# Accumulator joins as accumulating GpSimd transfers, two more quarters by block products, and two closings in one unit

## The chip, the cores and the metric

The kernel runs on one core of a Trainium2 chip. TensorE (PE in the profile; PEld is its weight load) multiplies matrices into PSUM, VectorE (DVE), ScalarE (ACT) and GpSimd (POOL) work element by element, and SyncE (SP) issues most transfers. Each engine takes its instructions strictly in the order in which they were written, and waits for semaphores where an instruction needs the result of another engine. The metric is the device time of one execution in microseconds (us).

## The reference

All arrays are bfloat16. `x` is 2048 tokens by 512, there are 32 heads of 128, and 2048 cached keys and values per head. The result is `x` plus the attention output times a gate.

```python
def _A_ref(x, k_cache, v_cache, wq, wo):
    B, Sq, D = x.shape
    H, Dh = 32, 128
    q = (x @ wq).reshape(B, Sq, H, Dh).transpose(0, 2, 1, 3)
    scores = jnp.einsum("bhqd,bhkd->bhqk", q, k_cache) * (Dh ** -0.5)
    p = _softmax(scores, axis=-1)
    o = jnp.einsum("bhqk,bhkd->bhqd", p, v_cache)
    return o.transpose(0, 2, 1, 3).reshape(B, Sq, H * Dh) @ wo
...
x = A_x
xn = _layernorm(x, axis=-1)
s = _A_ref(xn, A_k_cache, A_v_cache, A_wq, A_wo)
g = _silu(_B_ref(xn, B_w1, B_w2, B_w3, B_w4))
return x + s * g
```

`_B_ref` is an MLP mixer over the same tokens. The kernel computes its gate first and stores it in DRAM; the change doesn't touch it.

## The kernel before, in words

**Units and slots.** After the mixer the kernel runs 128 units. A unit is one head on one quarter of the queries (512 of 2048). Heads go in eight groups of four; the order is group, quarter, head, so unit number = 16 x group + 4 x quarter + head. A unit has eight slots. In each slot TensorE computes the scores of 256 keys (two matmuls of 512 columns into `ps_s`), ScalarE takes their exponential (`pT`, L447), and TensorE does the PV product of a slot ten slots back (`ps_o`). Every other piece of work is put at a slot by tables (`steps`, `o_steps`, `o_early`, `todo`) and written there by one loop, so an engine's order is fixed by hand. "117.3" below is slot 3 of unit 117.

**Row sums and normalisation.** VectorE adds up the exponentials of a unit (`add_first` L453, `add_half` L458, `add_next` L462, folds L466 and L470). One half of one addition (L458) is done by GpSimd at slot 6. The sums are turned by a DMA (`tT`), reduced, inverted, stored and broadcast by SP (`dr`, `rb`), and at slot 7 two units later VectorE multiplies `ps_o` by `rb` into `oT` (L524).

**Output projection.** When the four heads of a group are normalised for a quarter, `oT` (512 by 512) is multiplied by four heads' rows of `wo`, and added to f32 accumulators that stay in SBUF. This goes in one of two ways.

- *Direct*: `wo_slot` runs `wo_mm`, four matmuls of 512 columns for each tile of 128 tokens, and `wo_post` adds the PSUM bank `ps_wo` to the accumulator (L668). A quarter has four tiles. The bank is a single one, so the next tile waits for L668. `PLAN` names units in which these slots are set by hand: none in its first unit, then four tiles in three units.
- *Block products*: `wo_product` works on pairs of tiles. Operands are cut in halves both ways, and seven products in place of eight give the pair (`tw` and `so` are sums of weight and operand blocks); each product is two matmuls of 256 columns for 128 rows. `wo_take` adds PSUM to the accumulators four times a pair (L598), `o_sum` makes four operand sums a quarter (L573). `BLOCK` lists the quarters that are done so: of groups 0 to 6 all but the first of group 0 and the last two of group 6.

**Joins.** For block products the accumulators of a pair of tiles are one buffer `sa` of five pieces of 256 columns. Piece 3 holds a term that three of the four results share, summed over all groups. Once the last block product of a quarter is taken, `wo_join` adds piece 3 to pieces 2 and 4 in one VectorE operation and to piece 1 in another (L604). That is done for eight pairs.

**Closing tiles.** The last group's products are direct. For quarters 0 and 1 `fin_load` brings a tile's `x` and gate (`xl`, `gl`) through SP, and after the tile's last addition `y_last` multiplies the accumulator by the gate (L676), adds `x` (L678), and SP stores the tile. One tile is closed at slot 3 of each unit in which one is ready. For quarters 2 and 3 the accumulators are scaled by the gate ahead of the last product: `gate_load` brings the gate into a buffer that is free by then, `y_scale` multiplies (L636), and `y_add` adds `x` by an accumulating transfer of GpSimd from DRAM (L640). `LATER` is the unit after the last block quarter: 104 here. The joins, scalings and `PLAN` are placed relative to it.

Of the kernel before, what the change touches and what calls it, by code (L numbers as in the profile page):

```python
# [9 lines left out]
ALU = mybir.AluOpType  # L10
FP32 = mybir.dt.float32
BF16 = mybir.dt.bfloat16
# [5 lines left out]
def kernel(  # L18
# [15 lines left out]
    nc = tc.nc  # L34
    P = nc.NUM_PARTITIONS
# [3 lines left out]
    Sq, D = x2d.shape  # L39
# [5 lines left out]
    QT = Sq // 512  # L45
# [6 lines left out]
    NG = H // HG  # L52

    SPU = KC // 2
# [34 lines left out]
    qtp = ent(pool("qt", 6))  # L89
# [21 lines left out]
    def mm(out, lhsT, rhs, start, stop, **kw):  # L111
# [9 lines left out]
        out=ident[:], in0=diag[:], scalar1=0.0, scalar2=None, op0=ALU.is_equal))  # L121
# [5 lines left out]
    LATE = (QT - 2, QT - 1)  # L127
# [7 lines left out]
    def at(n, fn):  # L135
        todo[n].append(fn)
# [399 lines left out]
    def halves(x):  # L536
        return x.rearrange("p (a c) -> p a c", a=2)

    def sa_pair(qt, i):
        x = sp[qt, i] = pS.tile([P, 5, D // 2], FP32, tag="sacc", bufs=NT // 2, name="sacc")  # L540
        sacc[4 * qt + i], sacc[4 * qt + i + 2] = x[:, 0:3:2, :], x[:, 1:5:3, :]
        return x
# [5 lines left out]
    def sa_clear(qt, i):  # L548
        pin(nc.gpsimd.memset(sa_pair(qt, i)[:], 0.0))
# [49 lines left out]

    def wo_join(qt, i):  # L600
        sa = sp[qt, i]
        for out in (sa[:, 2:5:2, :], sa[:, 1:2, :]):
            n = 2 if out is not None and out.shape[1] == 2 else 1
            pin(nc.vector.tensor_tensor(  # L604
                out=out, in0=out, in1=sa[:, 3:4, :].to_broadcast([P, n, D // 2]), op=ALU.add))

    def gate_load(t, i):
        tag = ("tw0", "so2", "tw3", "so0", "so1", "so3", "tw1", "tw0")[i]
        gin[t] = pS.tile([P, D], BF16, tag=tag, bufs=2 if tag == "tw0" else 1, name="gin")[:]
        pin(nc.sync.dma_start(out=gin[t], in_=gates[t][:]))  # L610

    wog, sp, tw, so, wo_ps, gin = {}, {}, {}, {}, {}, {}
# [22 lines left out]
    def y_scale(t):  # L635
        pin(nc.vector.scalar_tensor_tensor(  # L636
            out=sacc[t], in0=sacc[t], scalar=0.5, in1=halves(gin[t]), op0=ALU.mult, op1=ALU.mult))

    def y_add(t):
        pin(nc.gpsimd.dma_start(out=sacc[t], in_=halves(xsrc[t]), accum_op=ALU.add))  # L640
# [31 lines left out]
    pair, last = {}, deque()  # L672
# [322 lines left out]
    pS = None  # L995
# [52 lines left out]
    def pv_run(n):  # L1048
        while pv_at[0] <= n - LAG:
            pv_slot(*divmod(pv_at[0], SPU))  # L1050
            pv_at[0] += 1

    def norm_queue(u):
        norm(u)
        gg, qq, hh = units[u]
        if hh == HG - 1 and (gg, qq) not in BLOCK:
            wo_todo.extend((gg, 4 * qq + ts) for ts in range(4))
# [5 lines left out]
    def wo_slot(part, n, each=2, **kw):  # L1063
        gg, t = wo_todo[0]
        if part < HG // each:
            wo_mm(gg, t, tuple(range(part * each, (part + 1) * each)), **kw)
            return
        wo_todo.popleft()
        wo_post(gg, t, n)
        if gg == NG - 1 and t % 4 < 3 and t + 1 not in fin and t // 4 not in LATE:  # L1070
            fin_load(t + 1)

    FIRST, LAST = 14, NU - 4
    BLOCK = [(g, qt) for g in range(NG - 1) for qt in range(QT)][1:-2]
    APART = range(2 * HG, NU - 3)
    pairs = range(FIRST, LAST + 1, 2)
    q_plan = defaultdict(list)
# [12 lines left out]
    o_steps, o_early = defaultdict(list), defaultdict(list)  # L1090
    for g, qt in BLOCK:
        u0 = ((g * QT + qt) * HG + 6) * SPU
# [13 lines left out]
            o_early[u0 + n].append((wo_sum, g, i))  # L1106
    for i, (qt, u) in enumerate((qt, qt * HG + 5 + j) for qt in range(1, QT) for j in range(2)):
        at(u * SPU + 6, lambda qt=qt, i=i: sa_clear(qt, i % 2))
    LATER = (BLOCK[-1][0] * QT + BLOCK[-1][1] + 1) * HG
    for u, qt, i in ((-7, 2, 0), (-4, 2, 1), (0, 3, 0), (1, 3, 1), (6, 0, 0), (10, 0, 1), (12, 1, 0), (14, 1, 1)):  # L1110
        o_steps[(LATER + u) * SPU + 3].append((wo_join, qt, i))
    for i, u in enumerate((10, 11, 12, 13, 14, 16, 18, 20)):
        n = (LATER + u) * SPU
        t = 4 * LATE[0] + i
        at(n - 2 * SPU + 4, lambda t=t, i=i: gate_load(t, i))
        at(n + 3, lambda t=t: y_scale(t))
        at(n + 6, lambda t=t: y_add(t))
    CATCH = {2 * HG * SPU + p: x for p, x in {
        0: ((0, "xa"),), 1: ((1, "xa"),), 2: ((2, "xa"),), 3: ((0, "xm"),), 4: ((1, "xm"),),
        5: ((2, "xm"), (0, "xa")), 6: ((1, "xa"),), 7: ((2, "xa"),)}.items()}  # L1120
    PLAN = {2 * HG: (), LATER + 6: (), LATER + 7: ((2, 0), (3, 1), (7, 2)), LATER + 8: ((1, 0), (3, 1), (4, 2), (6, 0), (7, 1)),
            LATER + 9: ((0, 2), (2, 0), (3, 1), (7, 2))}

# [28 lines left out]
    for n in range(UB * SPU):  # L1152
        u, p = divmod(n, SPU)
        if p == 0 and wo_box and u not in PLAN:
            wo_slot(4, n, each=1)
        s_slot(u, p)
        pv_run(n)
        for v, dcs in q_plan.get(n, ()):
            q_mm(v, dcs)
        run_steps(n, product)  # L1160
        run_steps(n, wo_product)
        run_steps(n, q_take)
        if p == 0 and 1 <= u:
            if u - 2 in TURN:
                turned_sums(u - 2)
                turned_recip(u - 2)
            run_all(o_early, n)
            if u not in third:
                add_last(u - 1)
        if p == 1 and u - 2 in TURN:  # L1170
            bcast(u - 2)
        if p == fold_at(u) and 1 <= u:
            for v in third.get(u, ()):
                add_last(u - 1)
                q_part(v, 1)
# [24 lines left out]
        if p == sum_p and 1 <= u and u - 1 not in TURN:  # L1200
            sums(u - 1)
        if p == sum_p + 1 and 1 <= u and u - 1 not in TURN:
            bcast(u - 1)
        if u == UA and p in (1, 2, 3):
            wo_slot(p - 1, n)
            if p == 3:
                fold_last(u - 1)
        for at_p, part in PLAN.get(u, ()):
            if at_p == p:
                wo_slot(part, n, each=2)  # L1210
        if p in at_wo and u not in PLAN and wo_todo and pS is not None and (p == at_wo[0] or wo_box):
            wo_slot(at_wo.index(p), n, each=each)
        if p == norm_p and u - 2 in TURN:
            norm_queue(u - 2)
        run_steps(n, q_part)
        if p == 4:
            run_all(o_early, n)
            add_first(u)
        run_all(o_steps, n)
        if p == 3 and last:  # L1220
            y_last(last.popleft())
        if p == 6:
            add_half(u, nc.gpsimd, LO) if u in APART else add_next(u, 2)
        pay()
        held_mm(n)
        for fn in todo.pop(n, ()):
            fn()
        if pS is None and not held:
            right.close()
            pS = right.enter_context(pool("pS", side="right", reuse_waits="tile"))  # L1230
            for tag, n in [("tw0", 2)] + [(x, 1) for x in ("tw1", "tw3", "so0", "so1", "so2", "so3")]:
                pS.tile([P, 2, D // 2], BF16, tag=tag, bufs=n, name="room")
            pS.tile([P, 2, 256], BF16, tag="xs", bufs=XS, name="room")
            pS.tile([P, 256], FP32, tag="tq", bufs=3, name="room")
# [3 lines left out]
    n = UB * SPU  # L1238
# [27 lines left out]
    def pv_to(k):  # L1266
# [29 lines left out]
        out=diag[:], in0=diag[:], scalar1=0.0, scalar2=None, op0=ALU.is_equal))  # L1296
# [98 lines left out]
```

## Time and profile before

| what | value |
|---|---|
| median of three runs | 1220.2 us (1220.19 to 1220.27) |
| the profiled execution | 1220.16 us |
| its span, from first to last instruction | 1218.4 us |
| busy: PE, DVE, ACT, POOL | 1207.3, 1103.2, 1096.6, 299.1 us |
| granted TensorE clock | 1.000 |

The page gives busy time per engine, the chain of work that ended last, and groups of instructions with their count, mean duration and the idle time before them. A row of the timeline gives a start, the time until the end, engine, line, operation and tiles; x2 or more means that neighbours of one kind are merged, and a bracket gives the engine's idle time ahead of it and what ended that. Operations overlap at their ends, so sums of durations come out some per cent above busy time.

### The profile page before, as it was taken

The page shows a single profiled execution, that of the slowest core. Times are in us where ns is not written, and L with a number is a line of the kernel's source. Part 1 is how long each engine was busy: PE and PEld are TensorE (multiplying, and loading weights), DVE is VectorE, ACT ScalarE, POOL GpSimd, SP SyncE. Part 2 cuts the span into 40 slices and gives each one's busy share as a digit, 9 for nine tenths or more (in the row PEclk, how much of TensorE's full clock was granted, in tenths as well). Part 3 has the DMA queues.
Part 4 walks back from the last instruction along what each step waited for, and adds up shares of the span by engine and source line. Part 5 has one row for each costly group of instructions (what it writes and reads, how often), then busy time and mean ns, then how long its engine had stood idle before and what let it go on. Part 6 is the DMA issues. An engine that isn't in the chain of part 4 may idle for free.

```text
span 1218.4 us, 18896 instructions
## 1 busy us (share of the span) xinstructions
PE 1207.3 (99%) x6556; PEld 676.8 (56%) x6678; DVE 1103.2 (91%) x1945; ACT 1096.6 (90%) x1241; POOL 299.1 (25%) x222
## 2 busy tenths in 40 slices
PE   9999999999999999999999999999999999999998
PEld 7466444555555555555555555555555555555555
DVE  8855789999999999999999999999999999989997
ACT  5444999999999999999999999999999999999996
POOL 5301001323222222222222222222222222233320
PEclk9999999999999999999999999999999999999999
DMA  8771133544334433344343443343344434445542
GB/s 179 176 158 55 40 70 79 96 93 91 82 87 83 104 69 89 83 96 91 75 87 88 99 78 80 87 98 79 85 87 87 105 66 92 84 102 111 122 113 66
DMA packets 248160, 113.08 MB, mean 93 GB/s; under 512 B 195328, under 2 KB 231296, under 8 KB 248064
## 3 DMA queue, kind: packets, MB, share of 16 engines
q1 hardware_dynamic: 244560, 107.21, 40.9%
q0 software_dynamic: 2944, 4.20, 1.5%
q8 instruction: 52, 0.85, 0.3%
q14 instruction: 44, 0.36, 0.2%
q10 hardware_dynamic: 560, 0.46, 0.1%
HBM read 69.60 MB, written 4.45 MB: 61 GB/s over the span
## 4 chain that ended last, share of the span: by engine, by line
PE 98%; issue 1%; ACT 0%; DVE 0%; DVEq 0%; ACTq 0%
PE ps_s L112 41%; PE ps_o L112 38%; PE ps_q L112 8%; PE ps_wo L112 8%; PE ps_m L112 3%; ACT pT L447 0%; PE ps_warm L112 0%; PE ps_oh L112 0%; DVE y L1257 0%; DVE tm L1250 0%; DVE tb L746 0%; PE ps_w L112 0%; DVEq L1390 0%; PE ps_r L112 0%; PE ps_sum L112 0%
## 5 line engine op out<-in xcount | busy, mean ns | idle before, releaser
L447 ACT ACTIVATE pT<-ps_s 128x1024 bf16<-128x1024 f32 x1016 | 1007.6, 1027 | 49.3 <-PE ps_s L112 23.7
L112 PE MATMUL ps_s<-qT,kT 128*128 128x512 bf16 (+1 forms) x2054 | 606.9, 377 | 0.2
L112 PE MATMUL ps_o<-pT,vb 128*128 128x512 bf16 x1885 | 568.7, 379 | 4.7
L458 POOL TENSOR_TENSOR acc<-acc,pT 128x1024 bf16<-128x1024 bf16 x117 | 248.7, 2126 | 728.7 <-ACT pT L447 357.2
L112 PEld LDWEIGHTS <-vb 128*128 128x128 bf16 x1984 | 194.0, 98 | 216.6
L112 PEld LDWEIGHTS <-kT 128*128 128x128 bf16 x2064 | 231.7, 113 | 93.5 <-issue 1.0
L462 DVE TENSOR_TENSOR acc<-acc,pT 128x2048 bf16<-128x2048 bf16 x137 | 167.7, 1224 | 21.1 <-ACT pT L447 5.1
L453 DVE TENSOR_TENSOR acc<-pT 128x2048 bf16<-128x2048 bf16 x127 | 154.8, 1219 | 8.1 <-ACT pT L447 8.0
L598 DVE TENSOR_TENSOR sacc<-ps_wo,sacc 128x512 f32<-128x512 f32 x200 | 123.4, 617 | 14.1 <-PE ps_wo L112 11.2
L466 DVE TENSOR_TENSOR acc<-acc 128x1024 bf16<-128x1024 bf16 x127 | 87.3, 687 | 2.4
L500 DVE TENSOR_REDUCE sm<-tT 128x4 f32<-128x512 bf16 x124 | 84.0, 677 | 5.3 <-DMA tT<-acc 4.9
L524 DVE TENSOR_TENSOR oT<-ps_o,rb 128x512 bf16<-128x512 f32 x127 | 86.5, 681 | 2.2 <-DMA rb<-dr 1.9
L458 DVE TENSOR_TENSOR acc<-acc,pT 128x1024 bf16<-128x1024 bf16 x117 | 79.8, 682 | 0.0
L112 PEld LDWEIGHTS <-wc 128*128 128x128 bf16 x448 | 43.8, 98 | 52.8
L112 PE MATMUL ps_wo<-wo_h,oT 128*128 128x256 bf16 (+1 forms) x295 | 70.7, 307 | 0.2
L112 PEld LDWEIGHTS <-oT 128*128 128x128 bf16 x428 | 41.6, 98 | 45.6
L301 ACT ACTIVATE h2T<-ps_s 128x1024 bf16<-128x1024 f32 x28 | 28.6, 1022 | 35.1 <-PE ps_s L112 35.1
L112 PEld LDWEIGHTS <-so 128*128 128x128 bf16 x400 | 39.1, 98 | 36.5
L470 DVE TENSOR_TENSOR acc<-acc 128x512 bf16<-128x512 bf16 x127 | 54.0, 425 | 4.3
L112 PEld LDWEIGHTS <-wq_h 128*128 128x128 bf16 x396 | 38.7, 98 | 34.3
L112 PE MATMUL ps_q<-xnT,wq_h 128*128 128x256 bf16 (+1 forms) x270 | 55.6, 291 | 0.1
L112 PEld LDWEIGHTS <-w_sb 128*128 128x128 bf16 x368 | 33.6, 98 | 28.9
(136 smaller groups left out, 934.4 us busy)
## 6 DMA issues: line engine op xcount, KB each, us to landing
rb<-dr SPq DMA_DIRECT2D x127, 256.0 KB, 3.8
vb<-in_A_v_cache_dram SPq DMA_DIRECT2D x62, 256.0 KB, 3.0
wq_h<-in_A_wq_dram SPq DMA_DIRECT2D x32, 128.0 KB, 2.5
wo_h<-in_A_wo_dram SPq DMA_DIRECT2D x32, 128.0 KB, 2.3
w_sb<-in_B_w_dram SPq DMA_DIRECT2D x8, 256.0 KB, 4.9
kT<-in_A_k_cache_dram SPq DMA_TRANSPOSE x128, 2.6
gate<-xall POOLq DMA_DIRECT2D x16, 128.0 KB, 2.8
sacc<-in_A_x_dram POOLq DMA_DIRECT2D x8, 256.0 KB, 4.6
```

Of the source, the lines that this page charges most:

```text
L112: pin(nc.tensor.matmul(out=out, lhsT=lhsT, rhs=rhs, start=start, stop=stop, **kw))
L301: pin(nc.scalar.activation(out=h2[c][:, f], in_=ps[:], func=ACT.Gelu_apprx_tanh))
L447: pin(nc.scalar.activation(out=s["pT"][-1][:, jj:jj + 2, :], in_=sps[:], func=ACT.Exp, scale=SCALE))
L453: pin(nc.vector.tensor_tensor(out=s["acc"][:], in0=s["pT"][0][:], in1=s["pT"][1][:], op=ALU.add))
L458: pin(eng.tensor_tensor(out=a[:, part, :], in0=a[:, part, :], in1=e[:, part, :], op=ALU.add))
L462: pin(nc.vector.tensor_tensor(out=a[:], in0=a[:], in1=st[u]["pT"][i][:], op=ALU.add))
L466: pin(nc.vector.tensor_tensor(out=a[:, 0:2, :], in0=a[:, 0:2, :], in1=a[:, 2:4, :], op=ALU.add))
L470: pin(nc.vector.tensor_tensor(out=a[:, 0, :], in0=a[:, 0, :], in1=a[:, 1, :], op=ALU.add))
L500: pin(nc.vector.tensor_reduce(out=sm[:], in_=s["tT"][:], axis=mybir.AxisListType.X, op=ALU.add))
L524: pin(nc.vector.tensor_tensor(out=to, in0=o, in1=rb, op=ALU.mult))
L598: pin(nc.vector.tensor_tensor(out=out, in0=ps, in1=out, op=ALU.add))
```

## The change

Three things change, and with them places in the tables. `wo_join` issues two accumulating transfers on GpSimd's queue, SBUF to SBUF, where VectorE did two additions. `BLOCK` takes in the last two quarters of group 6, so `LATER` becomes 112 and `PLAN` moves to units 118 to 121. And `y_last` also runs at slot 6 of unit 121. The joins are at units 106 to 119 in the order of quarters (before: 97 to 118). The scalings are at 115 to 124 (before: 114 to 124), with the gate loads two units ahead of them into other free buffers.

```diff
     def wo_join(qt, i):
         sa = sp[qt, i]
-        for out in (sa[:, 2:5:2, :], sa[:, 1:2, :]):
-            n = 2 if out is not None and out.shape[1] == 2 else 1
-            pin(nc.vector.tensor_tensor(
-                out=out, in0=out, in1=sa[:, 3:4, :].to_broadcast([P, n, D // 2]), op=ALU.add))
+        for out, n in ((sa[:, 2:5:2, :], 2), (sa[:, 1:2, :], 1)):
+            pin(nc.gpsimd.dma_start(out=out, in_=sa[:, 3:4, :].to_broadcast([P, n, D // 2]), accum_op=ALU.add))
 
     def gate_load(t, i):
-        tag = ("tw0", "so2", "tw3", "so0", "so1", "so3", "tw1", "tw0")[i]
-        gin[t] = pS.tile([P, D], BF16, tag=tag, bufs=2 if tag == "tw0" else 1, name="gin")[:]
+        tag = ("tw1", "tw3", "tw0", "qT", "qT", "so2", "so0", "so1")[i]
+        pl, n = (qtp, 5) if tag == "qT" else (pS, 2 if tag == "tw0" else 1)
+        gin[t] = pl.tile([P, D], BF16, tag=tag, bufs=n, name="gin")[:]
...
-    BLOCK = [(g, qt) for g in range(NG - 1) for qt in range(QT)][1:-2]
+    BLOCK = [(g, qt) for g in range(NG - 1) for qt in range(QT)][1:]
...
+    JOINS = ((-6, 0, 0), (-4, 0, 1), (-2, 1, 0), (0, 1, 1), (2, 2, 0), (4, 2, 1), (5, 3, 0), (7, 3, 1))
+    SCALES = ((8, 3, 3), (10, 4, 4), (9, 5, 5), (11, 6, 6), (12, 7, 7), (14, 7, 8), (13, 10, 10), (15, 12, 12))
...
-    for u, qt, i in ((-7, 2, 0), (-4, 2, 1), (0, 3, 0), (1, 3, 1), (6, 0, 0), (10, 0, 1), (12, 1, 0), (14, 1, 1)):
+    for u, qt, i in JOINS:
         o_steps[(LATER + u) * SPU + 3].append((wo_join, qt, i))
...
-        if p == 3 and last:
+        if (p == 3 or (u, p) == (LATER + 9, 6)) and last:
             y_last(last.popleft())
```

A row of SCALES is the tile, the unit of its scaling and the unit of its residual transfer, both counted from `LATER`. Lines behind the changed place stand one lower in the changed kernel (L676 is L675, L640 is L639).

TensorE at slots 2 and 3 of unit 111, where the direct tiles of group 6 began. Before, `oT` is the stationary operand and the four heads' `wo_h` stream 512 columns each:

```order
L112 LDWEIGHTS oT_12195
L112 MATMUL ps_wo_12639<-wo_h_10276,oT_12195 128x512
L112 LDWEIGHTS oT_12195
L112 MATMUL ps_wo_12639<-wo_h_10276,oT_12195 128x512
L112 LDWEIGHTS kT_11176
```

Now, at the same place, with the next slot's scores behind it:

```order
L112 LDWEIGHTS oT_12189
L112 MATMUL ps_wo_12639<-wo_h_10276,oT_12189 128x256
L112 LDWEIGHTS oT_12189
L112 MATMUL ps_wo_12639<-wo_h_10276,oT_12189 128x256
L112 LDWEIGHTS kT_11176
L112 MATMUL ps_s_12642<-qT_12369,kT_11176 128x512
L112 LDWEIGHTS kT_11176
L112 MATMUL ps_s_12642<-qT_12369,kT_11176 128x512
```

The direct tile with 512 columns a matmul is gone from here; a block product with 256 columns stands in its place, and the direct tiles of the last group come eight units later.

GpSimd in units 114 to 116. Before, only its half of the row sums (L458) and the residual transfers (L640) stand there, in units 114, 115 and 116:

```order
L458 TENSOR_TENSOR acc_12956<-acc_12956,pT_12951 128x1024
L640 DMA sacc_2900<-in_A_x_dram 128x2x256
L458 TENSOR_TENSOR acc_13053<-acc_13053,pT_13049 128x1024
L640 DMA sacc_3005<-in_A_x_dram 128x2x256
L458 TENSOR_TENSOR acc_13152<-acc_13152,pT_13147 128x1024
```

Now two joins (L603) stand among them, those of quarter 2's two pairs, `sacc_2900` and `sacc_3005`:

```order
L603 DMA sacc_2900<-sacc_2900 128x2x256
L603 DMA sacc_2900<-sacc_2900 128x256
L458 TENSOR_TENSOR acc_12969<-acc_12969,pT_12963 128x1024
L458 TENSOR_TENSOR acc_13071<-acc_13071,pT_13064 128x1024
L639 DMA sacc_2900<-in_A_x_dram 128x2x256
L603 DMA sacc_3005<-sacc_3005 128x2x256
L603 DMA sacc_3005<-sacc_3005 128x256
L458 TENSOR_TENSOR acc_13175<-acc_13175,pT_13171 128x1024
```

The second join stands behind a residual transfer and ahead of the row-sum addition of its unit.

VectorE in unit 121, from slot 4 on. Before, the addition of a tile of the last group (L668) follows the first row sums and the last part of a Q projection:

```order
L453 TENSOR_TENSOR acc<-pT 128x2048
L432 TENSOR_TENSOR qT<-ps_q,tq 128x512
L668 TENSOR_TENSOR sacc<-ps_wo,sacc 128x2x256
L524 TENSOR_TENSOR oT<-ps_o,rb 128x512
L500 TENSOR_REDUCE sm<-tT 128x4
```

Now the second closing of the unit, written at slot 6, stands ahead of that addition:

```order
L453 TENSOR_TENSOR acc<-pT 128x2048
L432 TENSOR_TENSOR qT<-ps_q,tq 128x512
L675 SCALAR_TENSOR_TENSOR gl<-sacc,gl 128x512
L677 TENSOR_TENSOR xl<-gl,xl 128x512
L667 TENSOR_TENSOR sacc<-ps_wo,sacc 128x2x256
L524 TENSOR_TENSOR oT<-ps_o,rb 128x512
```

Two operations have moved in ahead of the one that empties `ps_wo`, and of the normalisation behind it.

More of the change, by code (lines that the diff above doesn't have):

```diff
@@ L1108 @@
         at(u * SPU + 6, lambda qt=qt, i=i: sa_clear(qt, i % 2))
+    JOINS = ((-6, 0, 0), (-4, 0, 1), (-2, 1, 0), (0, 1, 1), (2, 2, 0), (4, 2, 1), (5, 3, 0), (7, 3, 1))
+    SCALES = ((8, 3, 3), (10, 4, 4), (9, 5, 5), (11, 6, 6), (12, 7, 7), (14, 7, 8), (13, 10, 10), (15, 12, 12))
     LATER = (BLOCK[-1][0] * QT + BLOCK[-1][1] + 1) * HG
-    for u, qt, i in ((-7, 2, 0), (-4, 2, 1), (0, 3, 0), (1, 3, 1), (6, 0, 0), (10, 0, 1), (12, 1, 0), (14, 1, 1)):
+    for u, qt, i in JOINS:
         o_steps[(LATER + u) * SPU + 3].append((wo_join, qt, i))
[L1112 to L1117, printed above, removed]
+    for i, (t, u, w) in enumerate(SCALES):
+        at((LATER + u - 2) * SPU + 4, lambda t=t, i=i: gate_load(t, i))
+        at((LATER + u) * SPU + 3, lambda t=t: y_scale(t))
+        at((LATER + w) * SPU + 6, lambda t=t: y_add(t))
     CATCH = {2 * HG * SPU + p: x for p, x in {
```

## The prediction

> **What bounds the kernel now.** I read the page's busy times and its chain first, then the stretch that the change touches (units 110 to 122, about 1053 to 1156 us), engine by engine.
>
> ```profile
> span 1218.4 us, 18896 instructions
> ...
> PE 1207.3 (99%) x6556; PEld 676.8 (56%) x6678; DVE 1103.2 (91%) x1945; ACT 1096.6 (90%) x1241; POOL 299.1 (25%) x222
> ...
> PE 98%; issue 1%; ACT 0%; DVE 0%; DVEq 0%; ACTq 0%
> ```
>
> The chain that ended last is 98% TensorE. A busy PE row is not yet a PE at its peak, since ends of matmuls are modelled, so I take the spacing of starts (TensorE in unit 104; a row with x2 is two matmuls one after the other):
>
> ```profile
> 999.66 0.59 PE L112 MATMUL ps_s<-qT,kT 128*128 128x512 bf16 x2
> 1000.09 0.59 PE L112 MATMUL ps_o<-pT,vb 128*128 128x512 bf16 x2
> 1000.52 0.38 PE L112 MATMUL ps_wo<-tw,oT 128*128 128x256 bf16 x2
> 1000.74 0.59 PE L112 MATMUL ps_s<-qT,kT 128*128 128x512 bf16 x2
> ```
>
> Two 512-column matmuls take 0.43 us from start to start, 0.215 us each; two of 256 columns take 0.22, some 0.11 each. Scores, PV and block product follow each other without a hole. So time goes by columns streamed, and what saves columns saves time.
>
> The second clock is the first copy of each pair of Q projections (`tq`, once in two units, at the same place of the even unit):
>
> ```profile
> 1002.34 0.38 ACT L416 ACTIVATE tq<-ps_q 128x256 f32<-128x256 f32 x1
> 1019.21 0.38 ACT L416 ACTIVATE tq<-ps_q 128x256 f32<-128x256 f32 x1
> ...
> 1052.95 0.38 ACT L416 ACTIVATE tq<-ps_q 128x256 f32<-128x256 f32 x1
> 1069.90 0.41 ACT L416 ACTIVATE tq<-ps_q 128x256 f32<-128x256 f32 x1
> 1087.87 0.41 ACT L416 ACTIVATE tq<-ps_q 128x256 f32<-128x256 f32 x1
> 1156.09 0.38 ACT L416 ACTIVATE tq<-ps_q 128x256 f32<-128x256 f32 x1
> ```
>
> These open units 104, 106, 110, 112, 114 and 122. A pair of units with block products takes 16.87 us, and the next two pairs take 33.74, as much each. The planned stretch (units 111 to 113, four direct tiles pressed together) makes its two pairs 16.95 and 17.97. From unit 110 to unit 122 it is 103.14 us.
>
> **The change, part by part.**
>
> *Two quarters by block products.* A direct quarter is 4 tiles by 4 heads: 16 matmuls of 512 columns, two quarters 32 x 0.215 = 6.88 us. By blocks a quarter is 2 pairs by 7 products by 2 matmuls: 28 of 256 columns, two quarters 56 x 0.11 = 6.16 us, or 56 x 0.1075 = 6.02. The saving is 0.72 to 0.86 us, all on the path.
>
> The clock rows give the same by another way. After the change units 110 to 117 are four pairs with block products, 4 x 16.87 = 67.48; the planned stretch stands at 119 to 121, with the same columns in every slot, so its two pairs again cost 16.95 + 17.97 = 34.92. Together 102.40 against 103.14: -0.74 us. From unit 122 on TensorE's rows are the same in both. I take -0.75.
>
> The Trainium skill speaks against this step. "TensorE: Matmul & The Clock Gate", section "Back-to-back issue gap", gives a sustained stream 81 ns at 128 columns and 131 ns at 512, so that half the columns cost far more than half; an estimate between its figures puts 256 columns at 98 ns, and the step would lose 56 x 0.098 - 32 x 0.131 = 1.3 us. The trace disagrees: 0.215 and 0.11 us in the stream of this very kernel, so the rows decide.
>
> *VectorE's share of it.* Rows by form:
>
> ```profile
> L598 DVE TENSOR_TENSOR sacc<-ps_wo,sacc 128x512 f32<-128x512 f32 x150 | 102.8, 685 | 9.4 <-PE ps_wo L112 7.2
> L598 DVE TENSOR_TENSOR sacc<-ps_wo,sacc 128x256 f32<-128x256 f32 x50 | 20.6, 412 | 4.7 <-PE ps_wo L112 4.0
> L573 DVE TENSOR_TENSOR so<-oT 128x512 bf16<-128x512 bf16 x50 | 19.0, 417 | 0.0
> L668 DVE TENSOR_TENSOR sacc<-ps_wo,sacc 128x512 f32<-128x512 f32 x16 | 11.0, 690 | 3.2 <-PE ps_wo L112 2.9
> ```
>
> Two quarters add 12 x 0.685 + 4 x 0.412 additions and 8 x 0.417 operand sums, 13.2 us, and drop 8 x 0.69 = 5.5.
>
> *The joins.* A join is two VectorE additions; the pair stands as one row:
>
> ```profile
> 1005.71 1.02 DVE L604 TENSOR_TENSOR sacc<-sacc 128x512 f32<-128x512 f32 x2
> ...
> 1013.78 1.02 DVE L604 TENSOR_TENSOR sacc<-sacc 128x512 f32<-128x512 f32 x2
> ```
>
> Eight of them are 8.2 us of VectorE gone, which with the step before leaves it 0.5 us lighter. I give that no gain: both rows lie in the pair from 1002.34 to 1019.21, which takes 16.87 us like the two pairs after it. VectorE had room for a join of 1.02 us beside the block products, so it has room for the scaling of 0.68 us that units 115 to 118 now carry each. In unit 119 two scalings stand together (1.36 us), where the last addition of a block product is just done.
>
> On GpSimd a join becomes two accumulating transfers. The nearest rows are the residual transfers, which accumulate the same 128 x 2 x 256 f32 from DRAM, and the gate stores:
>
> ```profile
> L640 POOL DMA_DIRECT2D sacc<-in_A_x_dram x8: 1061/1080/1156, 1095.7 to 1181.1; - x8
> ...
> DMA to landing us min/median/max: 3.5/4.6/4.8
> ```
> ```profile
> 1095.69 1.16 POOL L640 DMA_DIRECT2D sacc<-in_A_x_dram  x1
> ...
> 1118.68 2.12 POOL L458 TENSOR_TENSOR acc<-acc,pT 128x1024 bf16<-128x1024 bf16 x1 [4.56 <-ACT pT L447]
> ```
> ```profile
> L321 POOL DMA_DIRECT2D gate<-xall x16 | 8.9, 559 | 129.5 <-DVE xall L318 129.2
> ```
>
> So the two issues hold GpSimd between 2 x 0.56 = 1.1 and 2 x 1.16 = 2.3 us; I take 2.2, since both accumulate. Queued behind a join is GpSimd's half of the row-sum addition (L458), and VectorE's next addition waits for that. Where a residual transfer stands in the same unit the idle time before that addition is still 4.56 us at least, so 2.2 fits and the price is 0. Landing, 3.5 to 4.8 us a transfer, is needed by the scaling a unit (over 8 us) later at the earliest: 0 too. If the cover went, a join of 2.2 us would delay VectorE by 2.2.
>
> The Trainium skill, "SBUF — State Buffer", section "SBUF: two separate sides", warns that VectorE can lock GpSimd out while it writes descriptors, 3.1 us for a transfer of 0.62. By that figure a join would hold GpSimd 6.2 us, more than the 4.56. The trace does not show it: the eight issues took 1.06 to 1.16 us beside a busy VectorE.
>
> The transfers share the DMA engines with the broadcast of reciprocals (`rb`), which the normalisation waits for:
>
> ```profile
> DVE oT L524 <- DMA rb<-dr: 1.9, 4, 0.6
> ```
>
> That is 1.9 us in four waits of 127. More of these may come; they delay VectorE, not yet TensorE. I price them at 0.
>
> *Two closings in unit 121.* A closing is two VectorE operations (0.682 and 0.426 by their groups). The planned stretch now meets closings, which it did not in units 111 to 113. The rows of VectorE and TensorE at the old end of that stretch:
>
> ```profile
> L676 DVE SCALAR_TENSOR_TENSOR gl<-sacc,gl 128x512 bf16<-128x512 f32 x8 | 5.5, 682 | 0.0
> L678 DVE TENSOR_TENSOR xl<-gl,xl 128x512 bf16<-128x512 bf16 x8 | 3.4, 426 | 0.3
> ```
> ```profile
> 1082.68 1.23 DVE L453 TENSOR_TENSOR acc<-pT 128x2048 bf16<-128x2048 bf16 x1 [0.57 <-ACT pT L447]
> ...
> 1084.65 0.69 DVE L432 TENSOR_TENSOR qT<-ps_q,tq 128x512 bf16<-128x512 f32 x1 [0.74 <-PE ps_q L112]
> 1085.26 0.68 DVE L668 TENSOR_TENSOR sacc<-ps_wo,sacc 128x512 f32<-128x512 f32 x1
> ...
> 1088.16 0.38 PE L112 MATMUL ps_wo<-wo_h,oT 128*128 128x512 bf16 x1
> ...
> 1090.71 1.02 DVE L604 TENSOR_TENSOR sacc<-sacc 128x512 f32<-128x512 f32 x2
> ...
> 1092.26 1.22 DVE L453 TENSOR_TENSOR acc<-pT 128x2048 bf16<-128x2048 bf16 x1
> ...
> 1093.97 0.69 DVE L668 TENSOR_TENSOR sacc<-ps_wo,sacc 128x512 f32<-128x512 f32 x1 [0.50 <-PE ps_wo L112]
> ...
> 1095.72 0.38 PE L112 MATMUL ps_wo<-wo_h,oT 128*128 128x512 bf16 x1
> ```
>
> TensorE's next tile (1088.16, 1095.72) needs the one PSUM bank that L668 empties. Laid over these rows, the closing of 121.3 (1.1 us) falls into the idle 0.57 and 0.74. That of 121.6 stands ahead of the first L668, which then ends at 1087.04 instead of 1085.94, with 1088.16 needed. By the second L668 the closing of 122.3 has come as well (2.2 us) and the old join (1.0) has gone: 1.2 later, of which 0.5 was idle. It ends at about 1095.4 with 1095.72 needed. Price 0, but only 0.3 us of cover; without it the loss is what VectorE is further behind, an estimate of up to 1.2 us, once.
>
> *Gate loads and order of the scalings.* The loads change buffers that lie idle by then (operand sums and weights last read in unit 118 at the latest), with one exception read in the slot just before; their count is unchanged: 0. On SP the loads for tiles 2 to 4 of the last head group now stand behind the stores of closings in units 120 and 121, and the next unit's reciprocals are queued behind them. A load waits only for a store issued more than a slot earlier, so I give this 0 too and leave the doubt to the first rival.
>
> **Sum.** -0.75 against the profiled execution's 1220.16 us (span 1218.4) gives 1219.4; the median of the runs, 1220.2, stands 0.04 above that execution. What a measurement here can tell from no change I set at 0.2%, 2.44 us; so this forecast is "no change".
>
> **Rivals.**
>
> *Gain eaten near unit 121.* For it: 0.3 us of cover, SP's loads for the closings, `rb` landing later beside the joins. Against it: VectorE's idle time in the same rows. It gives back 0.4 to 1.5 us: 1219.8 to 1221. Still within 0.2%.
>
> *GpSimd too late: slower.* A join's issues hold GpSimd so long that its addition, then VectorE, then TensorE wait. The margins:
>
> ```profile
> 956.57 0.68 DVE L598 TENSOR_TENSOR sacc<-ps_wo,sacc 128x512 f32<-128x512 f32 x1
> ...
> 956.78 2.12 POOL L458 TENSOR_TENSOR acc<-acc,pT 128x1024 bf16<-128x1024 bf16 x1 [5.73 <-DVE acc L453]
> ...
> 958.13 0.38 PE L112 MATMUL ps_wo<-wo_h,so 128*128 128x256 bf16 x2
> ...
> 959.70 1.22 DVE L462 TENSOR_TENSOR acc<-acc,pT 128x2048 bf16<-128x2048 bf16 x1
> ```
>
> GpSimd ends at 958.90, VectorE wants it at 959.70 (0.8 us); L598 ends at 957.25, TensorE wants it at 958.13 (0.9). It decides from 4.56 + 0.8 + 0.9 = 6.3 us a join, against 2.2 expected. At 7 us, eight joins cost about 8 x 0.7 = 5.6, less 0.75: 1225. Against it stand the eight rows of about 1.1 us.
>
> *Half-width matmuls cost more than half.* It turns at 6.88 / 56 = 0.123 us; at 0.16 the loss is 2.1 us, 1222.3. The rows of 0.11 speak against it.
>
> *Faster by over 0.2%.* It would need 2.44 us of TensorE's time where the pairs show none: in the direct pair of units 118 and 119 PE is busy 17.02 of 17.07 us.
>
> ```profile
> 1121.04:1138.11 17.07, 17.02 (x87) 8.88 (x87) 16.31 (x28) 16.25 (x20) 5.83 (x4) 1.00 0.59 123
> ```
>
> **How the numbers follow.** Forecast 0.70; gain eaten 0.17; GpSimd too late 0.08; half-width matmuls, at their price of 2.1 us within the bound, 0.02; faster 0.03. Same: 0.70 + 0.17 + 0.02 = 0.89, of which I move 0.02 to slower and 0.01 to faster for what these rows may not show: same 0.86, slower 0.10, faster 0.04. The range goes from 1219.0 (0.86 saved, and 0.3 for what the pairs hide) to 1221.2, the end of the second case, leaving out the slow one.
>
> **What would show it right or wrong.** Right: the period of `tq` is 16.87 in units 110 to 117, PE's idle time before ps_wo stays near 0, GpSimd's transfer rows are 0.5 to 1.2 us. Wrong: transfer rows over 3 us and VectorE's L462 waiting for POOL; periods over 18 us at units 118 to 122; ps_wo of 256 columns spaced more than 0.123 us.

## The result and the profile after

| kernel | median | runs | ratio to before (95% interval) |
|---|---|---|---|
| before | 1220.23 us | 1220.19 to 1220.29 | |
| changed | 1226.66 us | 1224.62 to 1227.22 | 1.0049 (1.0039 to 1.0059) |

The change makes the kernel slower by 0.49%, some 6 us, and its runs spread over 2.6 us where those of before agree within 0.1 (within 1.2 in the later sets). The forecast was 1219.4. The profiled execution took 1225.65 us. The page of the changed kernel, the same parts as were shown of before, with the queue of GpSimd's transfers (packets, MB, share of the 16 DMA engines):

```profile
span 1223.8 us, 18980 instructions
...
PE 1208.3 (99%) x6580; PEld 677.8 (55%) x6702; DVE 1105.2 (90%) x1945; ACT 1096.9 (90%) x1241; POOL 316.3 (26%) x238
...
q0 software_dynamic: 6272, 7.34, 3.2%
...
PE 91%; DVE 5%; DMA 2%; issue 1%; ACT 0%; DVEq 0%; POOL 0%
```

TensorE was 98% of the chain that ended last; now VectorE and DMA carry 7% of it. Busy PE still reads 99%, which tells nothing. The clock of the pairs, `tq` in units 110 to 122, tells where the time is lost:

```profile
1053.04 0.38 ACT L416 ACTIVATE tq<-ps_q 128x256 f32<-128x256 f32 x1
1069.91 0.38 ACT L416 ACTIVATE tq<-ps_q 128x256 f32<-128x256 f32 x1
1086.78 0.38 ACT L416 ACTIVATE tq<-ps_q 128x256 f32<-128x256 f32 x1
1105.16 0.38 ACT L416 ACTIVATE tq<-ps_q 128x256 f32<-128x256 f32 x1
1123.70 0.38 ACT L416 ACTIVATE tq<-ps_q 128x256 f32<-128x256 f32 x1
1140.66 0.41 ACT L416 ACTIVATE tq<-ps_q 128x256 f32<-128x256 f32 x1
1159.04 0.38 ACT L416 ACTIVATE tq<-ps_q 128x256 f32<-128x256 f32 x1
```

The first two pairs take 16.87 us each, as forecast. The pairs of units 114 and 116 take 18.38 and 18.54 in place of 16.87, that of 120 18.38 in place of 17.97: 3.6 us against the forecast. From unit 122 to the end of the span it is 64.8 us where before has 62.3: another 2.5.

The first long pair has its cause in unit 114. SP's queue and GpSimd's, then VectorE and TensorE of the changed kernel:

```profile
1085.49 1.08 SPq L159 DMA_DIRECT2D vb<-in_A_v_cache_dram  x1
1086.67 0.40 SPq L508 DMA_DIRECT2D dr<-rc  x1
1090.71 0.32 SPq L512 DMA_DIRECT2D rb<-dr  x1
```
```profile
1085.35 2.14 POOL L603 DMA_DIRECT2D sacc<-sacc  x2
```
```profile
1091.28 0.69 DVE L598 TENSOR_TENSOR sacc<-ps_wo,sacc 128x512 f32<-128x512 f32 x1
1094.59 0.69 DVE L524 TENSOR_TENSOR oT<-ps_o,rb 128x512 bf16<-128x512 f32 x1 [2.63 <-DMA rb<-dr]
```
```profile
1100.26 0.38 PE L112 MATMUL ps_q<-xnT,wc 128*128 128x256 bf16 x2 [0.50 <-DVE qT L429]
...
1103.53 0.62 PE L112 MATMUL ps_s<-qT,kT 128*128 128x512 bf16 x2 [0.51 <-DVE qT L432]
```

The join's two transfers go out at 1085.35, a value load at 1085.49, and 1.3 us later the tiny store of the reciprocals, `dr` (2 KB). The broadcast `rb` reads what `dr` wrote, so SP can issue it only when `dr` has landed, at 1090.71, 4.0 us after its issue. `dr`'s median over the kernel is 1.5, but at this place it is long without a join too. SP's queue in the kernel with no joins and the closing at slot 7 (see the experiments):

```profile
1085.81 0.40 SPq L508 DMA_DIRECT2D dr<-rc  x1
1088.94 0.32 SPq L512 DMA_DIRECT2D rb<-dr  x1
```

There `rb` follows `dr` after 3.1 us. Counted from `tq` of unit 112, that kernel issues `dr` at 15.67 us and `rb` at 18.80, the changed one at 16.76 and 20.80. Of the 2.0 us by which `rb` goes out later, 0.9 are `dr`'s landing. The other 1.1 are there before: VectorE has waited 0.78 us for `rb` after the join of unit 112, and the value load's issue takes 1.08 us in place of 0.58.

VectorE stands 2.63 us before the normalisation, and TensorE waits for VectorE's Q copies. The groups of the page show the sum of such waits (before: 1.9 for `rb`, longest 0.6, and 4.9 for `tT`; with no joins 4.1 and 6.2, so the joins are only part of the rise):

```profile
L524 DVE TENSOR_TENSOR oT<-ps_o,rb 128x512 bf16<-128x512 f32 x127 | 86.6, 682 | 6.7 <-DMA rb<-dr 6.4
L500 DVE TENSOR_REDUCE sm<-tT 128x4 f32<-128x512 bf16 x124 | 84.0, 677 | 7.3 <-DMA tT<-acc 7.0
```

The loss behind unit 122 looks different. VectorE, GpSimd and TensorE there, where the second closing of unit 121 stands:

```profile
1157.27 2.29 DVE L675 SCALAR_TENSOR_TENSOR gl<-sacc,gl 128x512 bf16<-128x512 f32 x1
1159.60 0.42 DVE L677 TENSOR_TENSOR xl<-gl,xl 128x512 bf16<-128x512 bf16 x1
1159.94 0.68 DVE L667 TENSOR_TENSOR sacc<-ps_wo,sacc 128x512 f32<-128x512 f32 x1
```
```profile
1156.90 2.11 POOL L458 TENSOR_TENSOR acc<-acc,pT 128x1024 bf16<-128x1024 bf16 x1 [5.78 <-issue]
```
```profile
1160.67 0.38 PE L112 MATMUL ps_wo<-wo_h,oT 128*128 128x512 bf16 x1 [1.13 <-DVE sacc L667]
```

L675 takes 2.29 us where its group took 0.68. It started while GpSimd's half addition ran, and ended 0.55 us after that addition did (1159.56 against 1159.01). L667 came late by the 1.6 us that L675 took longer, and the next direct tile waited 1.13 us for the PSUM bank.

### The profile page after: what moved, and what is told of

Same layout as the page of the kernel before. It is cut to its first block, busy times and chain, and to the rows that moved or that the text cites. A ratio compares the mean times of both kernels' runs of the same rounds, so it can differ in the third digit from the quotient of the medians.

```text
span 1223.8 us, 18980 instructions
## 1 busy us (share of the span) xinstructions
PE 1208.3 (99%) x6580; PEld 677.8 (55%) x6702; DVE 1105.2 (90%) x1945; ACT 1096.9 (90%) x1241; POOL 316.3 (26%) x238
## 3 DMA queue, kind: packets, MB, share of 16 engines
q0 software_dynamic: 6272, 7.34, 3.2%
## 4 chain that ended last, share of the span: by engine, by line
PE 91%; DVE 5%; DMA 2%; issue 1%; ACT 0%; DVEq 0%; POOL 0%
PE ps_s L112 38%; PE ps_o L112 35%; PE ps_q L112 8%; PE ps_wo L112 7%; PE ps_m L112 3%; DMA tT<-acc 1%; DVE acc L462 1%; DVE acc L453 0%; DMA rb<-dr 0%; DVE sm L500 0%; DVE acc L466 0%; DVE acc L458 0%; DVE gl L675 0%; DMA dr<-rc 0%; DVE oT L524 0%
## 5 line engine op out<-in xcount | busy, mean ns | idle before, releaser
L458 POOL TENSOR_TENSOR acc<-acc,pT 128x1024 bf16<-128x1024 bf16 x117 | 248.7, 2126 | 716.0 <-DVE acc L453 368.4
L598 DVE TENSOR_TENSOR sacc<-ps_wo,sacc 128x512 f32<-128x512 f32 x216 | 133.5, 618 | 17.1 <-PE ps_wo L112 13.9
L458 DVE TENSOR_TENSOR acc<-acc,pT 128x1024 bf16<-128x1024 bf16 x117 | 80.1, 685 | 0.0
L112 PEld LDWEIGHTS <-so 128*128 128x128 bf16 x432 | 42.3, 98 | 39.5 <-issue 0.2
L112 PE MATMUL ps_wo<-wo_h,oT 128*128 128x256 bf16 (+1 forms) x279 | 61.7, 296 | 1.6 <-DVE sacc L667 1.1
```

The costliest lines, as they stand in the source:

```text
L112: pin(nc.tensor.matmul(out=out, lhsT=lhsT, rhs=rhs, start=start, stop=stop, **kw))
L458: pin(eng.tensor_tensor(out=a[:, part, :], in0=a[:, part, :], in1=e[:, part, :], op=ALU.add))
L598: pin(nc.vector.tensor_tensor(out=out, in0=ps, in1=out, op=ALU.add))
```

## The experiments

My theory (A) was that the joins' transfers delay the chain `dr`, `rb`, `tT`, and so VectorE and TensorE; the first rival (B) that two closings and the planned stretch crowd VectorE and SP in units 119 to 122. The letters that follow stand in the expectations. There are three sets of four kernels, each with runs of the kernel before beside it. In the table, "114 to 121" is the time from `tq` of unit 114 to that of unit 122 in the profiled execution (forecast 2 x 16.87 + 16.95 + 17.97 = 68.66), "rest" from there to the end of the span (before 62.3).

| kernel | median, us | ratio (95% interval) | 114 to 121 | rest |
|---|---|---|---|---|
| changed | 1226.66 | 1.0049 (1.0039 to 1.0059) | 72.3 | 64.8 |
| joins on VectorE | 1224.17 | 1.0029 (1.0018 to 1.0040) | 71.8 | 63.7 |
| early joins transfers, late on VectorE | 1223.74 | 1.0026 (1.0016 to 1.0037) | 71.0 | 64.3 |
| late joins only, as transfers | 1226.14 | 1.0043 (1.0027 to 1.0060) | 72.2 | 64.8 |
| joins as plain copies | 1223.35 | 1.0022 (1.0013 to 1.0032) | 70.0 | 64.6 |
| joins of few bytes | 1222.67 | 1.0017 (1.0008 to 1.0027) | 68.7 | 64.8 |
| no joins | 1221.13 | 1.0004 (0.9995 to 1.0013) | 68.7 | 63.7 |
| no joins, closing at slot 7 | 1220.04 | 0.9996 (0.9987 to 1.0005) | 68.7 | 62.3 |
| one join, closing at slot 7 | 1220.25 | 0.9999 (0.9990 to 1.0008) | 70.1 | 62.5 |
| closing at slot 7 | 1225.70 | 1.0039 (1.0026 to 1.0053) | 74.2 | 63.3 |
| one closing a unit | 1224.83 | 1.0036 (1.0024 to 1.0049) | 73.1 | 62.3 |
| no scalings in 115 to 118 | 1226.24 | 1.0039 (1.0027 to 1.0052) | 71.3 | 64.3 |
| before, joins as transfers | 1221.13 | 1.0006 (0.9997 to 1.0015) | | 62.3 |

**Joins back on VectorE.**

```diff
         for out, n in ((sa[:, 2:5:2, :], 2), (sa[:, 1:2, :], 1)):
-            pin(nc.gpsimd.dma_start(out=out, in_=sa[:, 3:4, :].to_broadcast([P, n, D // 2]), accum_op=ALU.add))
+            pin(nc.vector.tensor_tensor(
+                out=out, in0=out, in1=sa[:, 3:4, :].to_broadcast([P, n, D // 2]), op=ALU.add))
```

> The changed kernel with its eight joins back as VectorE additions, at the changed kernel's places; blocks, planned stretch and closings as changed. Theory A (the accumulating transfers delay the chain of small transfers dr, rb, tT, and with it VectorE and then TensorE): the loss goes, 1219.4 to 1221.0 us, and the longest wait of L524 for rb is back near 0.6 us (2.6 in the changed kernel). Rival B (two closings and the planned stretch crowd VectorE and SP in units 119 to 122, whoever does the joins): 1225 us or more, since VectorE now has 8.2 us more to do; units 120 and 122 stay above 9.4 us.

Measured 1224.17: between both, nearer to B's 1225, and the longest wait for `rb` is 1.2 us, not 0.6. The transfers are worse than the VectorE additions, but VectorE has no room either: the pairs of units 110 and 112 already take 17.14 and 17.13 us in place of 16.87. TensorE of this kernel, in the pair of unit 116 (19.22 us):

```profile
1112.12 0.38 PE L112 MATMUL ps_wo<-wo_h,so 128*128 128x256 bf16 x2 [0.87 <-DVE sacc L598]
...
1120.55 0.38 PE L112 MATMUL ps_wo<-wo_h,oT 128*128 128x256 bf16 x2 [0.68 <-DVE sacc L598]
```

Here a join stands on VectorE beside a scaling and block products in units 116 and 117, and TensorE waits for a block product's addition.

**The kernel before with transfers for joins, at its old places.**

```diff
-            pin(nc.vector.tensor_tensor(
-                out=out, in0=out, in1=sa[:, 3:4, :].to_broadcast([P, n, D // 2]), op=ALU.add))
+            pin(nc.gpsimd.dma_start(out=out, in_=sa[:, 3:4, :].to_broadcast([P, n, D // 2]), accum_op=ALU.add))
```

> The kernel before with nothing changed but the joins, which become accumulating transfers of GpSimd at their old places (units 97, 100, 104, 105, 110, 114, 116, 118). Theory A: slower than before by 2 to 6 us (1222 to 1226), lost in the units after the joins of 114, 116 and 118, where loads or residual transfers stand beside them; the four joins up to 105 cost nothing. Rival B: 1219.5 to 1220.5 us, as before.

Measured 1221.13, 0.7 us above before, with an interval that takes in no difference. So the same transfers cost almost nothing there, and theory A as written is wrong on its own: they cost where they meet something. VectorE of this kernel in unit 114, whose join falls on direct tiles:

```profile
1094.38 0.69 DVE L666 TENSOR_TENSOR sacc<-ps_wo,sacc 128x512 f32<-128x512 f32 x1 [1.43 <-PE ps_wo L112]
1095.85 0.69 DVE L524 TENSOR_TENSOR oT<-ps_o,rb 128x512 bf16<-128x512 f32 x1 [0.79 <-DMA rb<-dr]
```

`rb` is late here too, by 0.79 (`dr` takes 4.7 us, in the kernel before 3.6), but VectorE had just idled 1.43 us for TensorE: it is ahead, and the wait goes no further. The pair of unit 114 takes 17.01 us, as before.

**One closing a unit.** The kernel leaves out one tile's closing altogether, since the row of closings doesn't catch up.

```diff
-        if (p == 3 or (u, p) == (LATER + 9, 6)) and last:
+        if p == 3 and last:
```

> The changed kernel without the second closing of unit 121 (the tile closes one unit later at slot 3). Theory A: 1224.5 to 1227, at most 1.5 us off the changed kernel, and unit 122 alone is shorter. Rival B: most of the loss goes, 1219.5 to 1222.

Measured 1224.83, 1.8 us below the changed kernel. The rest of the span is back at 62.3, and units 114 to 121 stay long: two losses, not one. That is inside A's range, though a little more than the 1.5 us that A allowed. Since one closing is missing, what its place alone costs can't be read from this kernel.

**Early joins as transfers, late ones on VectorE.**

```diff
+            m = sa[:, 3:4, :].to_broadcast([P, n, D // 2])
+            if qt < 2:
+                pin(nc.gpsimd.dma_start(out=out, in_=m, accum_op=ALU.add))
+            else:
+                pin(nc.vector.tensor_tensor(out=out, in0=out, in1=m, op=ALU.add))
```

> The changed kernel with the joins of quarters 0 and 1 (units 106 to 112) left as transfers of GpSimd, those of quarters 2 and 3 (units 114 to 119) back on VectorE. Theory A in its narrow form (a transfer costs something only where loads or residual transfers stand beside it): within 0.5 us of the kernel with all joins on VectorE, 1219.4 to 1221. A in a wide form (every join costs about the same): half of the loss stays, about 1223. Rival B: 1225 or more.

Measured 1223.74, within 0.5 us of all joins on VectorE as the narrow form says, but not at its 1221. Its pairs up to unit 115 take 16.87 us, that of 116 takes 18.59: the late four on VectorE are what costs there, beside the closing.

**The second closing at slot 7**, behind the two operations of that slot which read PSUM.

```diff
-        if (p == 3 or (u, p) == (LATER + 9, 6)) and last:
+        if (p == 3 or (u, p) == (LATER + 9, 7)) and last:
```

> The changed kernel with the second closing of unit 121 at slot 7 in place of slot 6, behind the addition and the normalisation of that slot, which read PSUM. Theory C (L675 of that closing took 2.29 us in place of 0.68 because it reads two operands of SBUF while GpSimd's half addition L458 runs; it ended 0.55 us after L458 in each kernel so far): it takes 0.7 us again, or little more, and the 1.13 us that TensorE waits for L667 go; 1224.5 to 1225.5 us, 1.2 to 2.2 below the changed kernel. Rival D (a second closing costs by its 1.1 us of VectorE work alone, wherever it stands): within 0.5 us of the changed kernel, 1226 to 1227.

Measured 1225.70, 1 us below the changed kernel. The median alone doesn't decide between C and D, since the intervals overlap and units 114 to 121 came out longer in this execution; the rest of the span, 63.3 in place of 64.8, and the rows do. VectorE and GpSimd at the second closing, of this kernel first, then of the one with no joins and the same slot:

```profile
1160.23 1.10 DVE L675 SCALAR_TENSOR_TENSOR gl<-sacc,gl 128x512 bf16<-128x512 f32 x1
```
```profile
1158.66 2.12 POOL L458 TENSOR_TENSOR acc<-acc,pT 128x1024 bf16<-128x1024 bf16 x1 [5.23 <-ACT pT L447]
```
```profile
1153.06 0.68 DVE L667 TENSOR_TENSOR sacc<-ps_wo,sacc 128x512 f32<-128x512 f32 x1
...
1154.25 0.68 DVE L675 SCALAR_TENSOR_TENSOR gl<-sacc,gl 128x512 bf16<-128x512 f32 x1
```
```profile
1152.24 2.11 POOL L458 TENSOR_TENSOR acc<-acc,pT 128x1024 bf16<-128x1024 bf16 x1 [5.54 <-ACT pT L447]
```

In the first L675 still starts 0.55 us before GpSimd is done and ends 0.55 after it (1161.33 against 1160.78). In the second it starts 0.1 us before GpSimd's end (1154.35), at 1154.25, and takes its 0.68. L667, which reads one operand from PSUM, keeps its 0.68 in the middle of GpSimd's addition. So L675 waits for GpSimd and then still needs some half a microsecond.

The Trainium skill has this rule: "SBUF — State Buffer", section "Who interferes with whom", says that a VectorE instruction with two SBUF inputs contends with a GpSimd instruction that reads SBUF, and that the later one blocks until the first is done. The trace agrees: 2.29, 1.10 and 0.68 us for one and the same operation, by where it starts against L458.

**No joins.** The shared term of the block products is left out of the accumulators.

```diff
-    for u, qt, i in JOINS:
-        o_steps[(LATER + u) * SPU + 3].append((wo_join, qt, i))
```

> The changed kernel with no joins at all, neither on GpSimd nor on VectorE (the shared term of the block products is left out of the accumulators). Theory E (of the loss of 7.2 us against the forecast some 4 to 5 belong to the joins' transfers in the DMA queues, the rest to the closing at slot 6 and to scalings beside block products): 1221.5 to 1222.5. Rival A (all of it the transfers): 1219.4 to 1220.3. Rival F (VectorE is overfull in units 115 to 118 whatever the transfers do): above 1223.5.

Measured 1221.13, ratio 1.0004: the joins' transfers are 0.45% (1.0049 less 1.0004) or 5.5 us of the loss, a little more than E said (the time lies just below E's 1221.5, and above A's 1220.3). Units 114 to 121 take 68.7, to the hundredth what the forecast said without any loss. F is out: VectorE is not overfull by the block products and scalings alone.

**No scalings in units 115 to 118.** Tiles 8 to 11 aren't scaled.

```diff
-        at((LATER + u) * SPU + 3, lambda t=t: y_scale(t))
+        if i > 3:
+            at((LATER + u) * SPU + 3, lambda t=t: y_scale(t))
```

> The changed kernel without the four scalings of units 115 to 118 (tiles 8 to 11 aren't multiplied by half their gate); joins stay as transfers, the closing at slot 6. That is 4 x 0.68 = 2.7 us less VectorE work where the block products of group six run. Theory F (VectorE has no room for them beside block products, so that each late rb or tT goes through to TensorE): 2 to 3 us below the changed kernel, 1223.5 to 1224.7. Rival A (the waits for rb and tT alone decide): at most 0.7 us below, 1226 or more.

Measured 1226.24 (1223.65 to 1226.95): 2.7 us less work on VectorE bring 0.4 at the median, which is A's side. But the five runs spread over 3.3 us, and two of them lie in F's range, so this kernel alone decides little; F is out by the kernel with no joins.

**No joins, second closing at slot 7.** Both edits above together.

> The changed kernel with no joins at all and the second closing at slot 7. If the two causes add up, it stands as far below the kernel with no joins as the closing at slot 7 stands below the changed kernel. Theory E with C: 1219.5 to 1221. Rival F: above 1222, with units 115 to 118 still longer than 34.5 us together (33.74 forecast).

Measured 1220.04, some 1.0 us below the kernel with no joins, as the closing at slot 7 stood 1.0 below the changed kernel: at the medians the two causes add up, though each interval reaches about 1 us either way. The clock of the pairs:

```profile
1053.27 0.38 ACT L416 ACTIVATE tq<-ps_q 128x256 f32<-128x256 f32 x1
...
1087.01 0.38 ACT L416 ACTIVATE tq<-ps_q 128x256 f32<-128x256 f32 x1
1103.88 0.38 ACT L416 ACTIVATE tq<-ps_q 128x256 f32<-128x256 f32 x1
1120.75 0.38 ACT L416 ACTIVATE tq<-ps_q 128x256 f32<-128x256 f32 x1
1137.70 0.40 ACT L416 ACTIVATE tq<-ps_q 128x256 f32<-128x256 f32 x1
1155.67 0.40 ACT L416 ACTIVATE tq<-ps_q 128x256 f32<-128x256 f32 x1
```

102.40 us from unit 110 to 122, which is the number of the forecast for that stretch, with the rest as before (62.3). Its ratio, 0.9996, can't be told from 1.

**Plain copies of the same bytes.** The shared term overwrites the accumulators in place of being added.

```diff
-            pin(nc.gpsimd.dma_start(out=out, in_=sa[:, 3:4, :].to_broadcast([P, n, D // 2]), accum_op=ALU.add))
+            pin(nc.gpsimd.dma_start(out=out, in_=sa[:, 3:4, :].to_broadcast([P, n, D // 2])))
```

> The changed kernel with the joins' transfers as plain copies of the same bytes, without accumulating (so the shared term overwrites the three accumulators in place of being added). Theory A (bytes on the 16 DMA engines delay dr, rb and tT): 1225 to 1227, as the changed kernel. Rival G (the accumulation is what makes them slow; a plain copy has shorter packets and lands sooner): 1221 to 1223.

Measured 1223.35, just above G's range and below A's: plain copies cost 0.18% over no joins (2.2 us), accumulating ones 0.45%. At the medians more than half of the price is the accumulation.

**Few bytes.** Sixteen accumulating transfers of as many pieces, with 16 of 256 columns; the others aren't joined.

```diff
-            pin(nc.gpsimd.dma_start(out=out, in_=sa[:, 3:4, :].to_broadcast([P, n, D // 2]), accum_op=ALU.add))
+            pin(nc.gpsimd.dma_start(out=out[:, :, 0:16], in_=sa[:, 3:4, 0:16].to_broadcast([P, n, 16]), accum_op=ALU.add))
```

> The changed kernel with the same sixteen accumulating transfers, but of 16 columns in place of 256 for each piece (the other 240 columns aren't joined). GpSimd issues as many transfers with as many pieces; the bytes are a sixteenth. Theory A: 1221 to 1222.5, as with no joins. Rival H (what GpSimd does for the issue is the cost, by its own time or by keeping VectorE from SBUF): 1225 to 1227.

Measured 1222.67, just above A's end and far from H's. Units 114 to 121 are back at 68.7 with GpSimd's issues as long as ever. So most of it isn't the issuing; it is what the transfers do on the DMA engines. Some 1.5 us over no joins stay (0.13%, with intervals that overlap). In the trace they lie in the rest, 64.8 in place of 63.7, and whether the issues, the pieces or the bytes cost them is not shown. GpSimd's queue in three kernels: no joins, plain copies, few bytes (packets, MB, share of 16 engines; changed kernel: 6272, 7.34, 3.2%):

```profile
q0 software_dynamic: 2944, 4.20, 1.5%
```
```profile
q0 software_dynamic: 3968, 7.34, 2.3%
```
```profile
q0 software_dynamic: 6272, 4.39, 2.1%
```

Over no joins the accumulating transfers take 1.7% of the engines' time, plain copies of the same bytes 0.8%, and the few bytes 0.6%. The losses over no joins, 0.45, 0.18 and 0.13%, stand in the same order: they follow the time on the DMA engines, not the bytes alone.

**Only the four late joins.**

```diff
-    for u, qt, i in JOINS:
+    for u, qt, i in JOINS[4:]:
```

> The changed kernel with only the four joins of units 114 to 119, as transfers; the four of units 106 to 112 are left out. Theory A in its narrow form (a transfer costs where the chain dr, rb, tT has no room, which is from unit 114 on): 1225.5 to 1227, as the changed kernel. Wide form (every join costs about 0.7): 1223.5 to 1224.5.

Measured 1226.14, as the changed kernel: the joins of units 114 to 119 are enough for the joins' loss, and leaving out the four of 106 to 112 gains nothing that the runs show. The trace shows that these matter for the place. Without them VectorE waits 1.10 us for `rb` in unit 114 in place of 2.63, the pair of 114 takes its 16.87, and that of 116 takes 19.39.

**One join, that of unit 114**, with the closing at slot 7.

```diff
-    for u, qt, i in JOINS:
+    for u, qt, i in JOINS[4:5]:
```

> The changed kernel with a single join, the one of unit 114, as two transfers; all other joins are left out, and the second closing of unit 121 stands at slot 7. To be read against the kernel with no joins and the closing at slot 7 (1220.04). Theory A: unit 115 is longer again by 1 to 1.5 us (8.62 without joins, 10.13 in the changed kernel), and the whole 1221 to 1221.7. Rival (one late chain is made up for within a unit, and only joins that follow each other cost): unit 115 stays at 8.62, 1219.8 to 1220.4.

Neither fits. The median, 1220.25, is the rival's, but the runs go from 1219.54 to 1221.53, and in the profiled one, the slowest, units 114 to 121 took 70.1. Its pair of unit 114 is 0.23 us longer, and the next, in which no join stands, 1.19. Its VectorE there:

```profile
1093.69 0.69 DVE L524 TENSOR_TENSOR oT<-ps_o,rb 128x512 bf16<-128x512 f32 x1 [1.32 <-DMA rb<-dr]
...
1112.85 0.69 DVE L500 TENSOR_REDUCE sm<-tT 128x4 f32<-128x512 bf16 x1 [1.39 <-DMA tT<-acc]
```

The first wait is the join's. Counted from `tq` of unit 112, `dr` goes out at 15.7 us here, with no joins and with few bytes alike, and `rb` follows after 3.8, 3.1 and 3.1 us. The second wait comes 19 us later, at a unit with a residual transfer but no join. So a single late chain can be made up for or can grow, which goes with the spread of the changed kernel's runs; by what it grows is not shown.

How much VectorE can lose is seen by laying four traces side by side. VectorE in unit 114 with only the late joins, then with plain copies:

```profile
1092.96 0.69 DVE L524 TENSOR_TENSOR oT<-ps_o,rb 128x512 bf16<-128x512 f32 x1 [1.10 <-DMA rb<-dr]
```
```profile
1093.19 0.69 DVE L524 TENSOR_TENSOR oT<-ps_o,rb 128x512 bf16<-128x512 f32 x1 [1.15 <-DMA rb<-dr]
```

Waits of 1.10, 1.15, 1.32 (one join) and 2.63 us (changed) make this pair longer by 0.00, 0.04, 0.23 and 1.51: VectorE's lead here is an estimated 1.1 us, and what goes beyond it TensorE pays in full. In the next pair waits of 1.21 (plain copies) and 1.39 cost 0.89 and 1.19, so little lead is left.

No version was found that beats the kernel before: the one without joins, which lacks work, is only even with it.

## Why the prediction was wrong

- **Two quarters by block products, -0.75: right.** 102.40 us from unit 110 to 122 was forecast and is what the two kernels without joins show.
- **The Trainium skill's figure for 256 columns: the rows were the better guide.** The first pairs take 16.87 us in the changed kernel too.
- **Joins on GpSimd, the issue: right.** 2.2 us were put down, 2.14 and 2.53 stand in the traces; with few bytes the issues are as long and units 114 to 121 as short as without joins. The rival of a late GpSimd named a time near the result (1225) with the wrong mechanism; that it came near is luck.
- **The step that failed: "The transfers share the DMA engines with the broadcast of reciprocals (`rb`) ... I price them at 0."** They cost 5.5 us. The place was named and the price was not worked out. I looked at the bulk of the chain (`rb`, idle 1.9 us) and at the joins' own landing, which nobody needs soon. What counts is the chain `dr`, `rb`, which SP issues link by link: beside a join `dr` lands 3.8 to 4.0 us after its issue, at a place where it takes 3.1 without one, and a delay of one unit's chain reaches the next unit's. "They delay VectorE, not yet TensorE" holds up to a lead of some 1.1 us in unit 114; the changed kernel's 2.63 went beyond it, and behind that little lead was left. In the kernel before, where direct tiles stand, the same transfers cost almost nothing.
- **VectorE's share, room for scalings: right, by the kernel with no joins. That it had room for the joins, as a general statement: wrong**: all joins on VectorE, over none, cost 0.25% (1.0029 less 1.0004), 3 us, most of it in units 114 to 119.
- **Two closings, 0 with "only 0.3 us of cover, without it up to 1.2 us": the size.** Moving the second closing saves 1.0 us at the medians; by the traces the rest of the span is 2.5 us longer in the changed kernel, 1.4 of which stand without joins too (63.7 against 62.3). The sum was made with 0.682 for L675, its group's mean; beside GpSimd's L458 it takes 2.29.
- **Gate loads and SP's order, 0: nothing speaks against it**, since units 110 to 122 come out to the hundredth without joins.
- **The range** ended at 1221.2, at the price given to the first rival (whose own end was put at 1221). That rival named `rb` landing later beside the joins, but near unit 121 and at 0.4 to 1.5 us. The waits came from unit 114 on, and cost 5.5.

Left open: why a store of 2 KB waits behind the joins' packets (by engine, by queue or at SBUF), what makes a late chain grow from unit to unit, and what share of the 5.5 us each of the four late joins has. That each wait for `rb` or `tT` beside a join is caused by it is argued from the times of the rows, but for `dr` in unit 114, where kernels with and without the join stand side by side. That the joins' transfers cause the loss as a whole, and for the most part by their work on the DMA engines, is shown.

## What to carry to other kernels

A transfer that nobody waits for can still be on the path, if a chain of small transfers, each issued when the one before has landed, runs beside it: price it by how much later the smallest link lands, against the lead that its consumer has at that place. Time that is freed on an engine counts only where the engine is full; the joins of the kernel before stood where VectorE had room, so taking them off it freed nothing. And an operation's mean duration holds only for the neighbours it has had: look at what runs on the other engines at the new place.

## What the runs showed of the hardware

- An accumulating transfer within SBUF is dearer than a plain copy of the same bytes: 416 packets a join against 128 ((6272 - 2944) / 8 and (3968 - 2944) / 8), twice the DMA engines' time, and twice the issue on GpSimd. The issues of the changed kernel and of the one with plain copies (minimum, median, maximum in ns):

```profile
L603 POOL DMA_DIRECT2D sacc<-sacc x16: 1190/1395/1812, 1017.6 to 1133.0; - x16
```
```profile
L603 POOL DMA_DIRECT2D sacc<-sacc x16: 554/729/1155, 1017.7 to 1131.2; - x16
```

- A VectorE operation on two SBUF operands that started well inside GpSimd's addition ended 0.55 us after it, however long that was (L675 2.29, 1.98 and 1.10 us in the changed kernel, with no joins and with the closing at slot 7, in place of 0.68), while operations with an operand in PSUM beside it kept their time.
